# Storing two result rows from partitions 31 and 32, each row repeated over 32 array columns, in a decode kernel

## The chip, the cores and the metric

The kernel runs on one core of one Trainium2 chip. The metric is device time in microseconds (us) of one execution. Six runs of the kernel before lie between 401.40 and 401.75 us, so 0.1 us is about what single runs scatter by.

## The reference

One token goes through a layer norm and then through two branches whose results are added: attention with a cached K and V (32 query heads, 4 cache heads, 65,536 keys), and a small mixer with an MLP.

```python
def reference(A_x, A_k_cache, A_v_cache, A_wq, A_wo, B_x, B_w1, B_w2, B_w3, B_w4):
    x = A_x                                # [1, 1, 1024] bf16
    xn = _layernorm(x, axis=-1)
    return x + _A_ref(xn, A_k_cache, A_v_cache, A_wq, A_wo) + _B_ref(xn, B_w1, B_w2, B_w3, B_w4)
# _A_ref: softmax(q k^T / sqrt(128)) v, then @ wo
# _B_ref: x1 = x + gelu(LN(x) @ w1) @ w2 with shifted quarters; x1 + gelu(LN(x1) @ w3) @ w4
```

The result is one row of 1,024 bf16 numbers, 2 KB. The caches and weights are 170 MB, so nearly all the time goes into loading.

## The kernel before

All contributions to the result are added up in one PSUM tile, `psB`. The first 512 numbers lie in partition 0 and the other 512 in partition 32, because the two halves (`j` = 0 and 1) use two column groups of the TensorE array that work side by side: in the timeline below, two matmuls of 378 ns each are done in 0.38 us.

```python
    def row_acc(j, lhsT, rhs, start=False):                      # L220
        nc.tensor.matmul(psB[32 * j:32 * j + lhsT.shape[1], :], lhsT=lhsT, rhs=rhs, start=start, stop=False,
                         tile_position=(0, 32 * j), skip_group_check=True)
    ...
    for j in range(2):                                            # x itself: the only call with 32 columns
        row_acc(j, ident_f[0:1, 0:32], accx[0:1, 512 * j:512 * (j + 1)], start=True)
    ...
    def compute_w4(lo, hi):
        wt = st.tiles["w4"]
        for c in range(lo, hi):
            for j in range(2):
                row_acc(j, hT[:, c:c + 1], wt[:, D * c + 512 * j:D * c + 512 * (j + 1)])
    ...
    compute_v(NU - 1)                      # the last cache tile
    early = sum(W4_PIECES[:2])             # w4 lands in pieces of 6, 5, 6, 4, 3, 2, 1, 1 chunks
    compute_w4(0, early)
    project(HKV - 1)
    compute_w4(early, FC)

    out_t = ogpool.tile([64, 512], BF16, name="out_t", tag="og")
    nc.scalar.copy(out=out_t[:], in_=psB[0:64, :])                                # L485
    nc.scalar.dma_start(out=out[0, 0, :].rearrange("(j n) -> j n", j=2),          # L486
                        in_=out_t[:].rearrange("(a b) n -> a b n", b=32)[:, 0, :])
```

The call for x, with the first 32 columns of an identity as weights, writes x to the first partition of its group and zeros to the other 31.

Of the kernel before, what the change touches and what calls it, by code (L numbers as in the profile page):

```python
# [92 lines left out]
def kernel(  # L93
# [14 lines left out]
    nc = tc.nc  # L108
# [89 lines left out]
    ident_f = const.tile([P, P], F32, name="ident_f")  # L198
# [9 lines left out]
    for b in range(2):  # L208
        nc.gpsimd.tensor_copy(
            out=spread[:, 2 * b:2 * b + 2, :].rearrange("p r (a i) -> p r a i", a=4),  # L210
            in_=ident_f[:, 64 * b:64 * b + 64].rearrange("p (i r) -> p r i", r=2).unsqueeze(2).to_broadcast([P, 2, 4, 32]))
# [6 lines left out]
    psB = ps_B.tile([P, 512], F32, name="psB")  # L218

    def row_acc(j, lhsT, rhs, start=False):  # L220
        nc.tensor.matmul(psB[32 * j:32 * j + lhsT.shape[1], :], lhsT=lhsT, rhs=rhs, start=start, stop=False,  # L221
                         tile_position=(0, 32 * j), skip_group_check=True)

    x_t = ppool.tile([P, DC, 32], BF16, name="x_t", tag="p")
    for a in range(4):
        nc.vector.transpose(out=x_t[32 * a:32 * a + 32].rearrange("p c j -> p (c j)"),  # L226
                            in_=x_row[:, 256 * a:256 * (a + 1)].rearrange("p (i c) -> p c i", c=DC))
# [3 lines left out]
    def layernorm(src, tag):  # L231
# [39 lines left out]
                          in_=sel8[:].unsqueeze(2).to_broadcast([P, 8, 16]))  # L271
# [5 lines left out]
    accx = ppool.tile([1, D], F32, name="accx", tag="p")  # L277
    nc.vector.tensor_scalar(out=accx[:], in0=x_row[0:1, :], scalar1=ln_s1[0:1, 0:1], scalar2=ln_s2[0:1, 0:1],
                            op0=ALU.mult, op1=ALU.add)
    for j in range(2):  # L280
        row_acc(j, ident_f[0:1, 0:32], accx[0:1, 512 * j:512 * (j + 1)], start=True)

    def row_matmul(acc, rep, cols, widths):
        for c in range(DC):
# [44 lines left out]
    def compute_w12():  # L329
        wt = st.tiles["w12"][:, 0:2 * DC * D].rearrange("p (w c n) -> p w c n", w=2, c=DC)  # L330
        ps1 = ps_S.tile([P, SUBS, 512], F32, name="ps1", tag="sc")
        for c in range(DC):
            for q in range(2):
                nc.tensor.matmul(ps1[0:32, q, :], lhsT=xn2_rep[:, c, :], rhs=wt[:, 0, c, 512 * q:512 * (q + 1)],
                                 start=(c == 0), stop=(c == DC - 1), tile_position=(0, 0))
        h1 = ppool.tile([32, 2, 512], BF16, name="h1", tag="p")
        nc.scalar.activation(out=h1[:], in_=ps1[0:32, 0:2, :], func=ACTF.Gelu_apprx_tanh)
        for c in range(DC):
            for j in range(2):
                row_acc(j, g_col[:], wt[:, 1, c, 512 * j:512 * (j + 1)])  # L340
        st.done("w12")
# [102 lines left out]
    def project(g):  # L444
        wt = st.tiles["wo"][:].rearrange("p (g j n) -> p g j n", g=HKV, j=8)
        for j in range(8):
            for h2 in range(2):
                if g == HKV - 1:
                    row_acc(h2, oT[g][:, j:j + 1], wt[:, g, j, 512 * h2:512 * (h2 + 1)])
                    continue  # L450
                nc.tensor.matmul(tail["rows"][0:1, h2, :], lhsT=oT[g][:, j:j + 1],  # L451
                                 rhs=wt[:, g, j, 512 * h2:512 * (h2 + 1)], start=(g == 0 and j == 0),
                                 stop=(g == HKV - 2 and j == 7), tile_position=(0, 0))
# [21 lines left out]
    for g in range(HKV - 1):  # L475
# [8 lines left out]
    out_t = ogpool.tile([64, 512], BF16, name="out_t", tag="og")  # L484
    nc.scalar.copy(out=out_t[:], in_=psB[0:64, :])  # L485
    nc.scalar.dma_start(out=out[0, 0, :].rearrange("(j n) -> j n", j=2),  # L486
                        in_=out_t[:].rearrange("(a b) n -> a b n", b=32)[:, 0, :])

# [1 line left out]
_INS = ['A_x', 'A_k_cache', 'A_v_cache', 'A_wq', 'A_wo', 'B_x', 'B_w1', 'B_w2', 'B_w3', 'B_w4']  # L490
# [26 lines left out]
```

## Time and profile before

| | before |
|---|---|
| time, median of the first 3 runs | 401.73 us |
| span of the profiled execution | 399.7 us |
| bytes read, rate | 169.87 MB, 425 GB/s |
| last w4 piece landed, as the chain of waits has it | 396.90 us |
| copy from PSUM starts; store issue starts; span ends | 397.36; 397.97; 399.74 us |

In the profiles PE is TensorE, PEld its weight loads, DVE VectorE, ACT ScalarE and ACTq its queue, which issues DMAs. The page's busy times, and its row of DMA shares in 40 slices (9 means 90% or more):

```profile
PE 229.8 (57%) x1348; PEld 44.8 (11%) x854; DVE 209.0 (52%) x154; ACT 27.3 (7%) x35; POOL 5.4 (1%) x28
...
DMA  9998999999999999999999999999999999999995
```

No engine is busy much more than half the time, and the DMA engines are at 80% or more in every slice but the last. The kernel is bound by loading until the last piece of w4 lands at 396.90 us; only what follows the last load can shorten it by other means. The matmuls and weight loads of the changed line, from the list of one line's instructions (durations in ns are minimum, median, maximum; then first and last start in us):

```profile
L221 PEld LDWEIGHTS <-hT x56: 79/83/84, 385.5 to 396.9; 128*1 128x1 bf16 x56
L221 PE MATMUL psB<-big,hT x56: 376/378/379, 385.5 to 396.9; 128*1 128x512 bf16 x56
```

The end of the timeline (start in us, duration in us, engine, line, operation; in brackets the idle time before it and what ended it):

```profile
391.54 0.38 PE L221 MATMUL psB<-big,hT 128*1 128x512 bf16 x2
392.50 1.03 PE L221 MATMUL psB<-big,hT 128*1 128x512 bf16 x8 [0.58 <-DMA big<-in_B_w_dram]
...
396.94 0.38 PE L221 MATMUL psB<-big,hT 128*1 128x512 bf16 x2 [0.26 <-DMA big<-in_B_w_dram]
396.94 0.08 PEld L221 LDWEIGHTS <-hT 128*1 128x1 bf16 x1 [0.56 <-issue]
397.36 0.58 ACT L485 CAST out_t<-psB 64x512 bf16<-64x512 f32 x1 [29.43 <-PE psB L221]
397.97 0.59 ACTq L486 DMA_DIRECT2D out_dram<-out_t  x1
```

PE waits for the DMA at the last piece of w4. Then come two matmuls, one copy and one store, each waiting for the one ahead. The issue of the store keeps ScalarE's queue for 0.59 us, and another 1.17 us pass from its end to the end of the span. All of this lies in the open: nothing runs beside it.

Three stretches of the end, with the granted clock of TensorE in the third column from the right:

```profile
core 0: us, PE busy (x) PEld busy (x) DVE busy (x) ACT busy (x) POOL busy (x), PEclk, DMA share, GB/s
384.00:388.00 4.00, 3.17 (x22) 0.99 (x24) 3.35 (x7) 0.00 (x0) 0.00 (x0) 1.00 0.99 415
388.00:392.00 4.00, 3.92 (x38) 1.48 (x33) 0.49 (x2) 0.00 (x0) 0.00 (x0) 1.00 0.99 412
392.00:396.00 4.00, 2.19 (x18) 0.77 (x18) 0.00 (x0) 0.00 (x0) 0.00 (x0) 1.00 0.84 332
```

### The profile page before, as it was taken

How to read it: one execution, taken by the hardware profiler on the slowest of the kernel's cores; microseconds unless marked ns; L12 is line 12 of the kernel's file. 1: busy time of each engine (PE TensorE's matmuls, PEld its weight loads, DVE VectorE, ACT ScalarE, POOL GpSimd, SP SyncE). 2: the span in 40 equal slices, each digit the busy share in tenths (PEclk: the TensorE clock that was granted, in tenths of full speed). 3: DMA queues.
4: the chain of work that ended last, by engine and by line, in shares of the span. 5: the costliest groups of instructions: out<-in, count | busy, mean ns of one | idle time of the engine just before them, and what ended most of it. 6: DMA issues, size and time to landing. Idle time of an engine off the chain costs nothing.

```text
span 399.7 us, 2547 instructions
## 1 busy us (share of the span) xinstructions
PE 229.8 (57%) x1348; PEld 44.8 (11%) x854; DVE 209.0 (52%) x154; ACT 27.3 (7%) x35; POOL 5.4 (1%) x28
## 2 busy tenths in 40 slices
PE   0561960591579247832964296429453936494985
PEld 0210000000200110010101000201010002010241
DVE  0610010975196559644953795269349931985040
ACT  1001010003000200020002000200100020002000
POOL 2000000000000000000000000000000000000000
PEclk9996895697769587968895679679976986597999
DMA  9998999999999999999999999999999999999995
GB/s 420 420 448 384 436 485 439 426 420 420 415 427 426 446 472 421 426 420 426 433 428 466 439 420 426 415 446 426 446 448 426 420 426 402 430 469 426 397 421 227
DMA packets 4575, 170.01 MB, mean 425 GB/s; under 512 B 467, under 2 KB 469, under 8 KB 982
## 3 DMA queue, kind: packets, MB, share of 16 engines
q1 hardware_dynamic: 4560, 169.87, 98.7%
q8 instruction: 8, 0.13, 0.1%
q14 instruction: 1, 0.01, 0.0%
q10 hardware_dynamic: 6, 0.00, 0.0%
HBM read 169.87 MB, written 0.00 MB: 425 GB/s over the span
## 4 chain that ended last, share of the span: by engine, by line
DMA 52%; DVE 26%; PE 16%; ACT 3%; another core or an unknown queue 2%; issue 1%; DVEq 0%; ACTq 0%
DMA big<-in_A_k_cache_dram 31%; DVE big L357 19%; DMA big<-in_A_v_cache_dram 10%; PE sc L362 8%; PE oacc L412 6%; DMA big<-in_A_wq_dram 5%; DMA big<-in_B_w_dram 4%; DVE p_sb L383 3%; DVE mx L367 3%; ACT p_sb L380 3%; PE psq L287 1%; PE pm_mx L369 0%; DVE m L371 0%; PE pm_mx L376 0%
## 5 line engine op out<-in xcount | busy, mean ns | idle before, releaser
L362 PE MATMUL sc<-big,qdiag 128*128 128x512 bf16 x512 | 129.0, 413 | 66.8 <-DVE big L357 61.2
L357 DVE STREAM_TRANSPOSE big<-big 128x4096 f32<-128x4096 f32 x32 | 139.4, 4412 | 50.5 <-DMA big<-in_A_k_cache_dram 50.5
L412 PE MATMUL oacc<-big,p_sb 128*32 128x512 bf16 x512 | 43.0, 509 | 34.5 <-DVE p_sb L383 34.5
L367 DVE TENSOR_REDUCE mx<-sc 128x1 f32<-128x2048 f32 x8 | 18.3, 2292 | 29.8 <-PE sc L362 29.8
L362 PEld LDWEIGHTS <-qdiag 128*128 128x128 bf16 x128 | 13.2, 103 | 178.1 <-issue 145.8
L380 ACT ACTIVATE p_sb<-sc,nball 128x2048 bf16<-128x2048 f32 x8 | 15.7, 1967 | 220.6 <-DVE nball L378 220.6
L383 DVE STREAM_TRANSPOSE p_sb<-p_sb 128x2048 bf16<-128x2048 bf16 x8 | 18.5, 2312 | 18.0 <-ACT p_sb L380 18.0
L412 PEld LDWEIGHTS <-p_sb 128*32 128x32 bf16 x512 | 17.2, 124 | 57.4 <-DVE p_sb L383 35.1
L287 PE MATMUL psh<-big,ln_rep_b 128*32 128x512 bf16 (+1 forms) x64 | 12.4, 943 | 8.3 <-DMA big<-in_B_w_dram 8.3
L451 PE MATMUL o_acc<-big,oT 128*1 128x512 bf16 x48 | 12.0, 415 | 2.4 <-ACT p_sb L380 2.4
L369 PE MATMUL pm_mx<-ident_f,mx 128*1 128x128 f32 x8 | 2.4, 296 | 19.1 <-DVE mx L367 19.1
L326 DVE STREAM_TRANSPOSE h_row<-h_row 128x896 bf16<-128x896 bf16 x1 | 1.1, 1111 | 21.4 <-ACT h_row L325 21.4
L421 DVE SCALAR_TENSOR_TENSOR og<-oacc,wb,og 128x512 f32<-128x512 f32 x4 | 3.0, 746 | 16.2 <-PE oacc L412 16.2
L221 PE MATMUL psB<-big,hT 128*1 128x512 bf16 x56 | 7.4, 378 | 2.2 <-DMA big<-in_B_w_dram 2.1
L457 DVE COPY o_rows<-o_acc 1x1024 f32<-1x1024 f32 x1 | 1.2, 1212 | 12.8 <-PE oacc L412 12.8
L235 PE MATMUL pm_ln<-ln_rowsum_a,ones_f 128*128 128x1 f32 x2 | 0.6, 348 | 12.6 <-DVE ln_rowsum_a L233 12.6
L311 POOL COPY qdiag<-qx 32x32 bf16<-32x32 bf16 x16 | 3.3, 204 | 279.4 <-PE sc L362 250.3
L433 PE MATMUL pm_e<-ol,sel8big 128*128 128x129 f32 x8 | 2.3, 370 | 8.2 <-DVE ol L432 8.2
L226 DVE STREAM_TRANSPOSE x_t<-x_row 32x256 bf16<-32x256 bf16 x4 | 2.5, 616 | 8.2 <-DMA x_row<-in_A_x_dram 8.1
L287 PE MATMUL psq<-big,ln_rep_a 128*32 128x512 bf16 x64 | 5.6, 527 | 1.2 <-DMA big<-in_A_wq_dram 1.2
L376 PE MATMUL pm_mx<-ident_f,rep 1*128 1x1 f32 x8 | 1.8, 228 | 5.0 <-DVE rep L373 5.0
L299 DVE CAST q_row<-psq 128x512 bf16<-128x512 f32 x1 | 0.7, 692 | 7.5 <-PE psq L287 7.5
(95 smaller groups left out, 72.4 us busy)
## 6 DMA issues: line engine op xcount, KB each, us to landing
big<-in_A_wo_dram SPq DMA_DIRECT2D x1, 8192.0 KB, 37.2
big<-in_B_w_dram SPq DMA_DIRECT2D x1, 7168.0 KB, 38.2
big<-in_B_w_dram SPq DMA_DIRECT2D x2, 2048.0 KB, 46.4
big<-in_B_w_dram SPq DMA_DIRECT2D x2, 1536.0 KB, 27.3
big<-in_B_w_dram SPq DMA_DIRECT2D x1, 1280.0 KB, 24.1
big<-in_B_w_dram SPq DMA_DIRECT2D x1, 1024.0 KB
big<-in_B_w_dram SPq DMA_DIRECT2D x1, 768.0 KB, 30.8
big<-in_B_w_dram SPq DMA_DIRECT2D x1, 512.0 KB, 31.5
```

The costliest lines, as they stand in the source:

```text
L221: nc.tensor.matmul(psB[32 * j:32 * j + lhsT.shape[1], :], lhsT=lhsT, rhs=rhs, start=start, stop=False, tile_position=(0, 32 * j), skip_gro ...
L226: nc.vector.transpose(out=x_t[32 * a:32 * a + 32].rearrange("p c j -> p (c j)"), in_=x_row[:, 256 * a:256 * (a + 1)].rearrange("p (i c) -> ...
L287: nc.tensor.matmul(acc[32 * q:32 * q + 32, i, 0:n], lhsT=rep[:, c, :], rhs=cols(c, i, q), start=(c == 0), stop=(c == DC - 1), tile_positio ...
L311: nc.gpsimd.tensor_copy(out=qdiag[at, LEAD:].rearrange("p (x c) -> p x c", x=4)[:, :, 32 * a:32 * a + 8], in_=qx[at, :, 8 * g:8 * g + 8])
L357: nc.vector.transpose(out=words, in_=words)
L362: nc.tensor.matmul(sc[:, e, :], lhsT=qdiag[:, c0:c0 + P], rhs=cols[:, s, e, :, b2, :, r], start=(s == 0 and b2 == 0 and r == 0), stop=(s = ...
L367: nc.vector.reduce_max(out=mx[:], in_=sc[:].rearrange("p e n -> p (e n)"), axis=AX.X)
L380: nc.scalar.activation(out=p_sb[:], in_=sc[:], func=ACTF.Exp, bias=nball[:, b:b + 1], scale=SCALE, accum_out=group["lall"][:, b:b + 1])
L383: nc.vector.transpose(out=flat, in_=flat)
L412: nc.tensor.matmul(oacc[32 * q:32 * (q + 1), :], lhsT=pT[:, e, 32 * t:32 * (t + 1)], rhs=vt[:, :, e, t, :], start=(e == 0 and t < 4), stop ...
L421: nc.vector.scalar_tensor_tensor(out=og[:], in0=oacc[:], scalar=wb[:, 1:2], in1=og[:], op0=ALU.mult, op1=ALU.add)
L451: nc.tensor.matmul(tail["rows"][0:1, h2, :], lhsT=oT[g][:, j:j + 1], rhs=wt[:, g, j, 512 * h2:512 * (h2 + 1)], start=(g == 0 and j == 0), ...
```

## The change

The one column of weights is broadcast over 32 array columns. Then partitions 0 to 31 all hold the first half of the result and partitions 32 to 63 the second, and partitions 31 and 32, which lie side by side, hold both halves. The store takes those two.

```diff
     def row_acc(j, lhsT, rhs, start=False):
-        nc.tensor.matmul(psB[32 * j:32 * j + lhsT.shape[1], :], lhsT=lhsT, rhs=rhs, start=start, stop=False,
-                         tile_position=(0, 32 * j), skip_group_check=True)
+        nc.tensor.matmul(psB[32 * j:32 * j + 32, :], lhsT=lhsT.to_broadcast([lhsT.shape[0], 32]), rhs=rhs, start=start,
+                         stop=False, tile_position=(0, 32 * j), skip_group_check=True)
...
-        row_acc(j, ident_f[0:1, 0:32], accx[0:1, 512 * j:512 * (j + 1)], start=True)
+        row_acc(j, ident_f[0:1, 0:1], accx[0:1, 512 * j:512 * (j + 1)], start=True)
...
-                        in_=out_t[:].rearrange("(a b) n -> a b n", b=32)[:, 0, :])
+                        in_=out_t[31:33, :])
```

The number and order of instructions on each engine stay the same.

## The prediction

> **What bounds the kernel.** By the page, the DMA engines are 9 tenths busy or more in nearly all 40 slices, 425 GB/s over a 399.7 us span. The chain of waits is 52% DMA, 26% DVE and 16% PE, nearly all in the cache loop (L357, L362, L412). L221, the changed line, has (list of one line's instructions) 4 matmuls from 16.6 us, already 32 columns wide, 16 at 55 us, and 76 between 384.6 and 397 us. In that tail PE waits for pieces of w4: the timeline shows idle 0.58, 0.85, 0.45 and 0.26 us, each ended by the DMA. The chain ends: w4 landing 396.90, two matmuls 0.40, ACT copy 0.58 from 397.36, store issue 0.59 from 397.97, span end 399.74.
>
> **What the change does.** The instruction comparison gives the same rows on all five engines; only PE's operand shapes differ. No instruction, wait, byte or buffer is added or removed.
>
> 1. Matmuls write 32 partitions, not 1. Their time is set by 512 moving columns: 379 ns at 1x512 in L221, and 379 ns at 32x512 in L412 at 379 to 383 us, both at clock 1.0. Cost: 0.
> 2. Weight loads have 32 columns, not 1: 83 ns (128x1, L221) against 97 ns (128x32, L412), +14 ns each. With 72 bf16 loads in the tail, +1.0 us of busy load. The Trainium skill, "TensorE: Matmul & The Clock Gate", section "LDWEIGHTS (loading the stationary operand)", says P/1.2 ns for P columns, 26 ns more for 31; the trace says half, and decides. These loads run beside the other column group's matmul (one starts every 118 ns), so most is hidden. Even if none were, the catch-up from 388.6 to 391.9 us grows by 29 x 14 ns = 0.4 us, within the 0.58 us of idle after it. After the last landing one load stays exposed: about 0.015 us. The repeated column is read with stride zero, whose cost no trace here shows; if loads doubled to 166 ns, the end might be 0.2 us later.
> 3. ACT copies 64 partitions as before: 0.58 us.
> 4. The store reads partitions 31 and 32, not 0 and 32. It stays two 1 KB packets of about 45 ns, 36 ns apart, over 1 us after the issue began. The skill's "SBUF — State Buffer", section "Door 1: The DMA port swizzle", puts 0 and 32 on one port, 31 and 32 on two; so at most one packet time, some 0.04 us, is won. The rest is issue and completion, not bytes.
> 5. The 16 g_col matmuls at 55 us use two loads in all: no shift.
>
> **Sum.** +0.015 - 0.04 us: nothing. **Predicted 401.75 us, range 401.2 to 402.4.** The three runs before spread 0.13 us; another chip may differ more. Faster by over 2%: 0.005; within 2%: 0.985; slower: 0.01.
>
> **What would show it.** Right: L221's 32-column loads near 97 ns; its matmuls still 379 ns; the last PE waits still ended by w4's DMA, the first shrinking by 0 to 0.4 us; last landing to ACT copy and store issue unchanged within 0.1 us; two 1 KB store packets. Wrong: loads over 150 ns or the last PE wait gone; the granted clock (0.81 mean, 1.0 in the tail) lower; the store on one engine, or its completion moved by over 0.3 us.
>
> **What could make it wrong.** A slow stride-zero weight read, the clock throttle answering the extra columns, or the store's issue depending on the partition step. None reaches the cache loop, so even these should stay below 1 us.

## More of the kernel before

One helper (`close_on_the_store`) moves the wait for the final store to the very end of the program, so that the span closes 0.44 us after the store's last packet.

The experiments ran on three chips (e1 to e4, e5 to e8, e9 to e11), each time beside the kernel before.

## The result, and the profile after

| | before | after |
|---|---|---|
| median, 6 runs each, the same rounds | 401.62 us | 401.10 us |
| lowest and highest | 401.40, 401.75 | 400.92, 401.14 |
| ratio after to before, 95% interval | | 0.9986 (0.9973 to 0.9999) |
| span of the profiled execution | 399.7 us | 398.9 us |

A ratio here is the mean time of one kernel's runs over that of the other's of the same rounds, so it is not quite the ratio of the medians. The gain is 0.52 us by the medians, 0.13%: far below the 2% that would count as faster, yet the slowest run after is faster than the fastest run before. The prediction expected no gain, and its range began at 401.2 us, so the result lies 0.1 us outside it.

The lines of the changed line after, from the list of one line's instructions:

```profile
L221 PEld LDWEIGHTS <-hT x56: 92/97/151, 386.2 to 396.6; 128*32 128x32 bf16 x56
L221 PE MATMUL psB<-big,hT x56: 376/379/634, 386.2 to 396.6; 128*32 128x512 bf16 x56
```

The end of the timeline after:

```profile
392.35 3.96 PE L221 MATMUL psB<-big,hT 128*32 128x512 bf16 x32
...
396.56 0.39 PE L221 MATMUL psB<-big,hT 128*32 128x512 bf16 x2 [0.25 <-DMA big<-in_B_w_dram]
396.56 0.09 PEld L221 LDWEIGHTS <-hT 128*32 128x32 bf16 x1 [0.55 <-issue]
396.99 0.58 ACT L485 CAST out_t<-psB 64x512 bf16<-64x512 f32 x1 [29.44 <-PE psB L221]
397.60 0.26 ACTq L486 DMA_DIRECT2D out_dram<-out_t  x1
```

And the same three stretches:

```profile
384.00:388.00 4.00, 2.81 (x14) 0.72 (x14) 3.52 (x4) 0.00 (x0) 0.00 (x0) 0.76 0.99 415
388.00:392.00 4.00, 4.00 (x32) 1.78 (x30) 0.94 (x4) 0.00 (x0) 0.00 (x0) 0.81 0.99 413
392.00:396.00 4.00, 3.98 (x38) 1.66 (x35) 0.00 (x0) 0.00 (x0) 0.00 (x0) 1.00 0.82 324
```

Three things differ. First, the store's issue takes 0.26 us where it took 0.59 us. Second, the copy starts 0.37 us earlier, because the last piece of w4 landed 0.38 us earlier. Third, PE is busy from 392.35 to 396.3 us with no wait for the DMA in between, at a lower clock just before. A reader who had only these two profiles could tell two stories: the store got cheaper, or the repeated columns changed PE's pace and the clock. The profiled spans differ by 0.9 us and the medians by 0.5 us, so some of the difference between these two profiles must be scatter.

### The profile page after: what moved, and what is told of

It reads as the page before. It is cut to its first block, busy times and chain, and to the rows that moved or that the text cites. A ratio compares the mean times of both kernels' runs of the same rounds, so it can differ in the third digit from the quotient of the medians.

```text
span 398.9 us, 2547 instructions
## 1 busy us (share of the span) xinstructions
PE 232.8 (58%) x1348; PEld 45.1 (11%) x854; DVE 209.0 (52%) x154; ACT 27.3 (7%) x35; POOL 5.3 (1%) x28
## 4 chain that ended last, share of the span: by engine, by line
DMA 58%; DVE 20%; PE 18%; ACT 2%; issue 1%; DVEq 0%; ACTq 0%
DMA big<-in_A_k_cache_dram 34%; DVE big L357 14%; DMA big<-in_B_w_dram 14%; DMA big<-in_A_v_cache_dram 11%; PE sc L362 7%; PE oacc L412 5%; PE psh L287 3%; DVE p_sb L383 2%; DVE mx L367 2%; ACT p_sb L380 2%; PE ps L334 1%; PE psB L221 1%; PE pm_mx L369 0%; DVE m L371 0%; DVE ol L432 0%
## 5 line engine op out<-in xcount | busy, mean ns | idle before, releaser
L412 PE MATMUL oacc<-big,p_sb 128*32 128x512 bf16 x512 | 43.9, 511 | 34.5 <-DVE p_sb L383 34.5
L451 PE MATMUL o_acc<-big,oT 128*1 128x512 bf16 x48 | 13.0, 440 | 2.4 <-ACT p_sb L380 2.4
L221 PE MATMUL psB<-big,hT 128*32 128x512 bf16 x56 | 8.3, 430 | 0.3 <-DMA big<-in_B_w_dram 0.3
L287 PE MATMUL psq<-big,ln_rep_a 128*32 128x512 bf16 x64 | 6.4, 585 | 1.3 <-DMA big<-in_A_wq_dram 1.3
```

Source lines behind the costliest of these rows:

```text
L221: nc.tensor.matmul(psB[32 * j:32 * j + 32, :], lhsT=lhsT.to_broadcast([lhsT.shape[0], 32]), rhs=rhs, start=start, stop=False, tile_positio ...
L287: nc.tensor.matmul(acc[32 * q:32 * q + 32, i, 0:n], lhsT=rep[:, c, :], rhs=cols(c, i, q), start=(c == 0), stop=(c == DC - 1), tile_positio ...
L412: nc.tensor.matmul(oacc[32 * q:32 * (q + 1), :], lhsT=pT[:, e, 32 * t:32 * (t + 1)], rhs=vt[:, :, e, t, :], start=(e == 0 and t < 4), stop ...
L451: nc.tensor.matmul(tail["rows"][0:1, h2, :], lhsT=oT[g][:, j:j + 1], rhs=wt[:, g, j, 512 * h2:512 * (h2 + 1)], start=(g == 0 and j == 0), ...
```

## The experiments

The theories:

- A: the store's issue and start are cheaper because its two partitions are side by side. A1: the step of one partition matters. A2: what matters is that 31 and 32 are on different ports, as the Trainium skill has it ("SBUF — State Buffer", section "Door 1: The DMA port swizzle": partitions 0 to 3 and 32 to 35 are on one port, 28 to 31 on another).
- B: the repeated columns changed PE's pace, the clock or the landing of w4.
- C: scatter.

The measure that tells them apart best is not the total but the tail, from the start of the copy to the end of the span. It leaves out when w4 landed, which moves by 0.45 us between profiles (the copy starts at 396.99 to 397.44 us over all of them) in no order that follows the change. The issue is the instruction with which an engine's queue hands a DMA over; a packet is one piece that is then moved, here one row of 1 KB. The table is made from the trace: its instruction records and, for the packets, the records of the DMA queue that ScalarE issues to.

| kernel | columns | partitions stored | step | issue, ns | issue start to first packet, us | gap of the two packets, ns | copy start to span end, us | median, us |
|---|---|---|---|---|---|---|---|---|
| before | 1 | 0, 32 | 32 | 595 | 1.24 | 36 | 2.38 | 401.62 |
| after | 32 | 31, 32 | 1 | 262 | 0.75 | 4 | 1.87 | 401.10 |
| e1 | 32 | 0, 32 | 32 | 588 | 1.23 | 36 | 2.36 | 401.62 |
| e2 | 1 | 31, 32 | 1 | 262 | 0.75 | 2 | 1.86 | 401.12 |
| e3 | 1 | 0, 1 | 1 | 267 | 0.74 | 36 | 1.88 | 401.10 |
| e4 | 32 | 0, 36 | 36 | 699 | 1.35 | 6 | 2.45 | 401.77 |
| e5 | 32 | 30, 32 | 2 | 687 | 1.33 | 3 | 2.44 | 401.78 |
| e6 | 32 | 30, 33 | 3 | 697 | 1.35 | 9 | 2.46 | 401.80 |
| e7 | 32 and 1 | 31, 32 | 1 | 269 | 0.76 | 2 | 1.87 | 401.22 |
| e8 | 1 | 0; 32 (two stores) | none | 243; 308 | 0.72 | | 2.17 | 401.49 |
| e9 | 32 | 0, 33 | 33 | 707 | 1.35 | 35 | 2.47 | 401.89 |
| e10 | 1 | 0; 32 (two stores) | none | 233; 322 | 0.72 | | 1.99 | 401.28 |
| e11 (the change again) | 32 | 31, 32 | 1 | 262 | 0.75 | 3 | 1.86 | 401.21 |

The kernel before had medians of 401.63 us (beside e1 to e4), 401.67 (e5 to e8) and 401.63 (e9 to e11). All kernels but e2 and e3 gave correct results. The intervals of the ratios of e2, e7, e10 and e11, given below, reach or just cross 1, so they alone do not prove a gain; but in each of these and in e3 the slowest run is faster than the fastest of the nine runs of the kernel before beside it. Theory C falls with this.

### e1: the repetition alone

```diff
-                        in_=out_t[31:33, :])
+                        in_=out_t[:].rearrange("(a b) n -> a b n", b=32)[:, 0, :])
```

(against the change)

> Repetition alone: rows repeated over 32 columns as in the change, store from partitions 0 and 32 as before. Theory A (the store's issue got cheaper because its two partitions lie side by side; after minus before is -0.5 us): no gain, ratio to before 0.9997 to 1.0004, store issue near 0.595 us, first store packet 1.24 us after the issue began, the two packets 35 ns apart. Theory B (the 32-column matmuls changed PE's pace, the clock or the landing of the last w4 piece, and that gave the 0.5 us): ratio near 0.9986 with the slow store issue. Theory C (noise between compilations or runs): nothing systematic in either.

Measured: 401.62 us, ratio 1.0000 (0.9986 to 1.0014). The end of its timeline:

```profile
396.63 0.39 PE L221 MATMUL psB<-big,hT 128*32 128x512 bf16 x2 [0.26 <-DMA big<-in_B_w_dram]
...
397.06 0.58 ACT L485 CAST out_t<-psB 64x512 bf16<-64x512 f32 x1 [29.47 <-PE psB L221]
397.67 0.59 ACTq L486 DMA_DIRECT2D out_dram<-out_t  x1
```

With all the repetition and the old store, the gain is gone and the issue takes 0.59 us again. This profile has the early landing of w4 as well (copy at 397.06 us), and still its span ends at 399.4 us: the early landing is not what the medians show. Theory B falls, as far as it explains the time.

### e2: the store alone

```diff
-                        in_=out_t[:].rearrange("(a b) n -> a b n", b=32)[:, 0, :])
+                        in_=out_t[31:33, :])
```

(against the kernel before; partition 31 holds zeros, so half of the result is wrong)

> Store alone: the kernel before, with partitions 31 and 32 stored; partition 31 holds zeros, so the first half of the result is wrong on purpose. Theory A: the whole gain, ratio 0.9983 to 0.9991, store issue near 0.262 us, first packet 0.75 us after the issue began. Theory B: ratio near 1.0000. Weight loads 83 ns as before under both.

Measured: 401.12 us, ratio 0.9987 (0.9975 to 1.0000). The whole gain comes without a repeated column. The lines of its timeline and of its stretches:

```profile
397.28 0.58 ACT L485 CAST out_t<-psB 64x512 bf16<-64x512 f32 x1 [29.48 <-PE psB L221]
397.89 0.26 ACTq L486 DMA_DIRECT2D out_dram<-out_t  x1
```

```profile
384.00:388.00 4.00, 2.67 (x15) 0.58 (x15) 3.31 (x4) 0.00 (x0) 0.00 (x0) 0.91 1.02 427
388.00:392.00 4.00, 4.00 (x26) 1.44 (x24) 1.22 (x5) 0.00 (x0) 0.00 (x0) 0.67 0.98 409
392.00:396.00 4.00, 4.00 (x40) 1.62 (x38) 0.00 (x0) 0.00 (x0) 0.00 (x0) 1.00 0.83 328
```

The second fence answers the other question that the profile after raised. With one-column weights, too, the clock falls to 0.67 in this profile and PE works from 388 to 396 us without a pause. e6 and e11, with 32 columns, were granted 1.00 in all three stretches. So the missing waits after go with the lowered clock, and that comes without repeated columns too. Whether repetition makes it more frequent is not shown: 5 of 7 profiles with 32 columns had a lowered clock in these stretches, and 1 of 5 with one column (e7, with both, left out). The wait at the last piece (0.20 us here, 0.25 after, 0.26 before) outlives it either way.

### e3: side by side on one port

```diff
-                        in_=out_t[:].rearrange("(a b) n -> a b n", b=32)[:, 0, :])
+                        in_=out_t[0:2, :])
```

(against the kernel before; the second half of the result is wrong)

> The kernel before, with partitions 0 and 1 stored (second half of the result wrong on purpose, zeros). They are side by side and, by the skill's port table, on one port, as 0 and 32 are. Theory A1 (the step of one partition matters): issue 0.26 us and ratio 0.9983 to 0.9991, as with 31 and 32. Theory A2 (two different ports matter): issue 0.595 us, ratio near 1.0000.

Measured: 401.10 us, ratio 0.9986 (0.9974 to 0.9999).

```profile
396.99 0.58 ACT L485 CAST out_t<-psB 64x512 bf16<-64x512 f32 x1 [29.43 <-PE psB L221]
397.60 0.27 ACTq L486 DMA_DIRECT2D out_dram<-out_t  x1
```

The two packets do follow each other by 36 ns, as with 0 and 32, yet the issue is the cheap one and the gain is whole. The ports are not its cause; A1 stands (the step, or what goes with it: see the end of the account below) and A2 falls.

### e4: two ports, 36 partitions apart

```diff
-                        in_=out_t[31:33, :])
+                        in_=out_t[0:37:36, :])
```

(against the change)

> The change's repeated rows, with partitions 0 and 36 stored: a correct result from two different ports by the skill's table, but 36 partitions apart. A1 (step of one): issue 0.595 us, ratio near 1.0000. A2 (ports): issue 0.26 us, ratio 0.9983 to 0.9991.

Measured: 401.77 us, ratio 1.0004 (0.9992 to 1.0017).

```profile
397.21 0.58 ACT L485 CAST out_t<-psB 64x512 bf16<-64x512 f32 x1 [29.59 <-PE psB L221]
397.82 0.70 ACTq L486 DMA_DIRECT2D out_dram<-out_t  x1
```

The gap of the packets is 6 ns, so the two ports are there, and the gain is not. The issue is even 0.1 us longer than at a step of 32, which no theory had expected.

### e5 and e6: steps of two and three

```diff
-                        in_=out_t[31:33, :])
+                        in_=out_t[30:33:2, :])     # e5
+                        in_=out_t[30:34:3, :])     # e6
```

(against the change)

> The change with partitions 30 and 32 stored (step of two; correct). By the runs so far the store's issue took 0.262 to 0.267 us at a step of one, 0.59 at 32, 0.70 at 36. Theory D1 (only a step of one is cheap): issue 0.55 us or more, ratio near 1.0000. Theory D2 (the cost grows with the distance): issue between 0.26 and 0.35 us and the gain of 0.5 us kept, ratio near 0.9987.

> The change with partitions 30 and 33 stored (step of three; correct). If the difference between 0.59 us at a step of 32 and 0.70 us at 36 is that 32 is a power of two, the issue takes about 0.70 us here and 0.59 us at a step of two. D2 (distance): under 0.35 us here. D1 alone says only: 0.55 us or more, ratio 1.0000 to 1.0005.

Measured: 401.78 us, ratio 1.0005 (0.9992 to 1.0019), and 401.80 us, ratio 1.0005 (0.9989 to 1.0020). The store lines, of e5 and then of e6:

```profile
397.71 0.69 ACTq L486 DMA_DIRECT2D out_dram<-out_t  x1
```

```profile
397.85 0.70 ACTq L486 DMA_DIRECT2D out_dram<-out_t  x1
```

A step of two costs as much as a step of 36. So it is not the distance (D2 falls) but whether the partitions are neighbours. The guess that a power of two saves the 0.1 us falls with it: two is a power of two, and its issue takes 687 ns.

### e7: only one row repeated

```diff
     def row_acc(j, lhsT, rhs, start=False):
+        if j == 0:
+            lhsT = lhsT[:, 0:1].to_broadcast([lhsT.shape[0], 32])
...
-                        in_=out_t[:].rearrange("(a b) n -> a b n", b=32)[:, 0, :])
+                        in_=out_t[31:33, :])
```

(against the kernel before)

> Partitions 31 and 32 stored, but only the first row repeated over 32 columns, the second left one column wide (correct). Theory A: the full gain, ratio 0.9983 to 0.9991, no different from the whole change, as the matmuls are off the end's path. If repetition costs something at the end, this is faster than the change by up to its one exposed load, 0.015 us, which these rounds cannot resolve.

Measured: 401.22 us, ratio 0.9988 (0.9976 to 1.0001). The second half's row is in partition 32 anyway, so only the first half needs repeating. The result is correct and the gain the same within the scatter.

### e8: two stores of one partition

```diff
-    nc.scalar.dma_start(out=out[0, 0, :].rearrange("(j n) -> j n", j=2),
-                        in_=out_t[:].rearrange("(a b) n -> a b n", b=32)[:, 0, :])
+    nc.sync.dma_start(out=out[0, 0:1, 512:1024], in_=out_t[32:33, :])
+    nc.scalar.dma_start(out=out[0, 0:1, 0:512], in_=out_t[0:1, :])
```

(against the kernel before)

> The kernel before, with two stores of one partition each, row 0 issued by ScalarE and row 32 by SyncE at the same time (correct; no repetition). If one partition, having no step, is issued as fast as two neighbours, each issue takes about 0.26 us, the first packet comes 0.75 us after it, and the ratio is near 0.9990 (the second semaphore at the end may cost 0.1 to 0.2 us). If it is as slow as the load of x, which is one partition and took 0.52 us to issue, there is little or no gain, ratio 0.9995 to 1.0005.

Measured: 401.49 us, ratio 0.9996 (0.9982 to 1.0009), so about a third of the gain, where a ratio near 0.9990 was expected for short issues. Its end:

```profile
core 0 of [0], span 399.5 us
...
397.33 0.58 ACT L485 CAST out_t<-psB 64x512 bf16<-64x512 f32 x1 [29.55 <-PE psB L221]
397.93 0.31 SPq L486 DMA_DIRECT2D out_dram<-out_t  x1
397.94 0.24 ACTq L487 DMA_DIRECT2D out_dram<-out_t  x1
```

Both issues are short, and the last packet ends at 398.755 us. From there 0.74 us (399.497 - 398.755) pass to the end of the span, where e11 has 0.44 us (399.057 - 398.617). The loss is in how the program closes, not in the stores.

### e9: step 33 on one port

```diff
-                        in_=out_t[31:33, :])
+                        in_=out_t[0:34:33, :])
```

(against the change)

> The change with partitions 0 and 33 stored (step 33; by the skill's port table both on port 0, as 0 and 32 are; correct). So far the issue took 0.59 us for the pair on one port (0 and 32) and 0.69 to 0.70 us for pairs on two ports (30 and 32, 30 and 33, 0 and 36). If ports make that 0.1 us: issue 0.59 us here and the two packets 36 ns apart. If the step of 32 is itself special: issue 0.69 to 0.70 us; the packets should still be 36 ns apart. Ratio to before 1.0000 to 1.0006 in both.

Measured: 401.89 us, ratio 1.0006 (0.9992 to 1.0019). The issue takes 707 ns although both partitions are on one port (gap 35 ns). So ports do not make the 0.1 us between the steps of 32 and 36 either. Why a step of 32 is cheaper than the other steps tried, all but the step of one, stays open.

### e10: two stores, waited for together, and e11: the change again

e10 is e8 with the closing helper waiting for both stores at the end:

```diff
-    store = next(i for b in reversed(blocks) for i in reversed(b.instructions) if i.opcode == "DMACopy")
-    stored = {u.id for u in store.sync_info.on_update}
+    stores = [i for b in reversed(blocks) for i in reversed(b.instructions) if i.opcode == "DMACopy"][:2]
+    stored = {u.id for store in stores for u in store.sync_info.on_update}
...
-    assert len(final) == 1 and not end.sync_info.on_update
+    assert len(final) == 2 and not end.sync_info.on_update
```

(against e8)

> The kernel before with one single-partition store on ScalarE and one on SyncE, as e8, but the last engine waits for both landings together, where e8 waited for the SyncE one ahead of the closing barrier. Correct. Theory: e8's stores landed as early as the change's and lost 0.27 us after the landing, in the closing sequence; with a joint wait the gain returns, ratio 0.9983 to 0.9992, span end about 0.45 us after the last landing. If the end stays 0.7 us after the last landing, the loss lies elsewhere and the ratio stays near 0.9996.

> The change itself once more, on the same chip and in the same rounds as e10. Theory A: ratio 0.9983 to 0.9991, store issue 0.26 us. Whichever of e10 and this is faster by more than 0.1 us of median is the better version; I expect them within 0.1 us of each other.

Measured: e10 401.28 us, ratio 0.9992 (0.9978 to 1.0005); e11, the change itself, 401.21 us, ratio 0.9989 (0.9977 to 1.0002). In e10, 0.52 us pass from the last packet to the end, against 0.74 us in e8: the joint wait brought most of the loss back (0.45 us was expected), and without any repeated column the result comes within 0.1 us of the change. It does not beat it. The end of e11, where the clock was 1.00 as in the profile before:

```profile
391.58 0.38 PE L221 MATMUL psB<-big,hT 128*32 128x512 bf16 x2
392.33 1.04 PE L221 MATMUL psB<-big,hT 128*32 128x512 bf16 x8 [0.36 <-DMA big<-in_B_w_dram]
...
396.77 0.39 PE L221 MATMUL psB<-big,hT 128*32 128x512 bf16 x2 [0.27 <-DMA big<-in_B_w_dram]
396.77 0.09 PEld L221 LDWEIGHTS <-hT 128*32 128x32 bf16 x1 [0.56 <-issue]
397.20 0.58 ACT L485 CAST out_t<-psB 64x512 bf16<-64x512 f32 x1 [29.33 <-PE psB L221]
397.81 0.26 ACTq L486 DMA_DIRECT2D out_dram<-out_t  x1
```

This is the fair partner of the profile before. The wait ahead of 392.3 us is 0.36 us where it was 0.58 us, and the wait ahead of the last piece is unchanged. But the heavier weight loads hardly took part in that: PE reached this wait at 391.97 us, where it was 391.92 us before, and the awaited piece had landed 0.18 us earlier (392.328 against 392.505). From the first matmul of this tail (384.60 and 384.57 us) to the wait PE took 7.37 us, against 7.36 us before. Thus about 0.01 us of the loads' extra time shows even here, and none at the end.

## Why the prediction was wrong

**Point 1 (matmul time) was right.** The median is 379 ns at 32 columns and 378 ns at one.

**Point 2 (weight loads) was right.** Loads went from 83 to 97 ns, the predicted 14 ns. The doubt about a column read with stride zero is settled: at full clock (e11, e6) no load took over 97 ns; the 151 ns in the profile after came with a lowered clock, as did 128 ns for one-column loads in e2. The first wait shrank by 0.22 us at equal clock (e11), within the predicted 0 to 0.4 us, but that is luck: 0.18 us of it is an earlier landing of w4, and the loads account for about 0.01 us. e1 shows that the repetition as a whole costs nothing that five runs can see.

**Point 3 (copy) was right:** 0.58 us in every profile.

**Point 4 (store) failed.** The prediction counted the packets and found 0.04 us, and that part was right: 31 and 32 are served 4 ns apart where 0 and 32 are 36 ns apart. But it went on: "The rest is issue and completion, not bytes", and took that rest for fixed. The completion was fixed: 0.44 us before and 0.45 us after pass from the last packet to the end of the span. The issue was not. With neighbouring partitions the issue takes 262 ns, not 595, which is 0.33 us, and the first packet follows the end of the issue after 0.49 us (0.754 - 0.262), not 0.65 us (1.242 - 0.595), which is 0.16 us more. Together 0.49 us, and with the closer packets the tail is 2.38 - 1.87 = 0.51 us shorter: all of the 0.52 us between the medians. The term "-0.04" in the sum should have been about -0.5. The prediction had named "the store's issue depending on the partition step" among what could make it wrong, but gave it no number. Its own sign of being wrong, a completion of the store moved by over 0.3 us, came: from the start of the issue to the end of the span it is 1.26 us after and was 1.77 us before.

**Point 5 was not tested by itself;** e1, which has the same 32-column matmuls at 55 us, shows no cost in total, and the trace after has the two loads there that it named.

**The sum** was thus wrong by one term. Of the 0.65 us between the predicted 401.75 and the measured 401.10 us, 0.52 us is this term and 0.13 us is the kernel before, whose median was 401.62 us in these rounds. That the change would stay within 2% was right.

What is shown: a store of two neighbouring partitions is issued in 0.26 to 0.27 us, and one with any other step tried in 0.59 to 0.71 us, whatever the ports and the repeated columns (e1 to e6, e9); and this, with the 0.16 us by which the first packet follows the issue sooner, is the gain in time.

What is not shown is which property of the store makes its issue short. The kernels of all runs were built once more, without a chip. In the built programs the store's DMA instruction carries a mark, `ant_dge_precooked`, wherever it reads neighbouring partitions or only one (after, e2, e3, e7, e8, e10, e11), and nowhere else (before, e1, e4, e5, e6, e9). Between the kernel before and e2, the partitions read and this mark are all that differs; in the kernel before, the store is the only one of 31 DMAs without it. So the step and the mark change together in every run, and no experiment keeps one and changes the other: the 0.33 us may belong to the mark, which is set when the program is built, and not to the partitions as such. The mark is not all either, since the load of x from one row has it and takes about 0.5 us to issue in every profile, where ScalarE's one-partition store takes 0.23 to 0.24 us. That is unexplained, and so is why a step of 32 takes 0.59 us where 2, 3, 33 and 36, unmarked like it, take about 0.70 us.

## What to carry to other kernels

At the end of a kernel the last store stands in the open, so look at how long its issue takes and how long after it the first packet moves, and not only at its bytes; in this kernel a store of two partitions was cheap to issue when they were neighbours, and the result can be laid out for that at the cost of work that another engine has slack for. Two separate one-partition stores on two queues do nearly as well, if the program waits for both of them in the last place. Compare the built instructions too: a small change of an access pattern can change more of them than its step. And before a difference between two profiles is explained, hold it against a third: the copy, which follows the last load, began at times 0.45 us apart, nearly the whole effect, while the part from the copy to the end was 1.86 to 1.88 us in all five kernels with neighbouring partitions.

## What the Trainium skill lacked or had wrong

- "DMA: Bandwidth & Descriptors", section "Latency and other measured facts", gives one figure, about 600 ns, for the first byte of a DMA issued from SyncE or ScalarE. For this 2 KB store the first packet came 0.74 to 0.76 us after the issue began with neighbouring partitions and 1.23 to 1.35 us after it otherwise. That this depends on the step between partitions, or on a mark that goes with it, is on none of the pages read: the issue took 262 to 269 ns at a step of 1, 588 to 595 at 32, and 687 to 707 at 2, 3, 33 and 36.
- "TensorE: Matmul & The Clock Gate", section "LDWEIGHTS (loading the stationary operand)", gives P/1.2 ns for P columns, from which an estimate is 26 ns more for 32 columns than for one; the profiles show 97 ns against 83 ns at full clock, 14 ns more.
- "SBUF — State Buffer", section "Door 1: The DMA port swizzle", is borne out: pairs on one port by its table (0 and 32, 0 and 1, 0 and 33) had packets 35 or 36 ns apart, pairs on two ports (31 and 32, 30 and 32, 30 and 33, 0 and 36) 2 to 9 ns. Nothing was found wrong there.
